# Turning k and r of one tile together: identity products on quarters of the TensorE array in place of whole-array transposes

## The chip, the cores and the metric

One core of a Trainium2 chip runs the whole program. The metric is the device time of one execution in microseconds (us), as the median of several runs.

## The reference, cut to what matters

Two blocks run one after the other. The first is an RWKV-6 recurrence over 4 batches, 8 heads, 768 steps and a head size of 48; the second is a layer norm with a two-layer MLP and a residual on the 384 joined head outputs.

```python
for t in range(S):                                  # S = 768
    cur = einsum('bhd,bhe->bhde', u * k[t], v[t])
    y[t] = einsum('bhd,bhde->bhe', r[t], state + cur)
    state = w[t][..., None] * state + einsum('bhd,bhe->bhde', k[t], v[t])
x = y as (B, S, 384)
xn = (x - mean) / sqrt(var + 1e-6) * g_ln
out = x + relu(xn @ w_ch1) @ w_ch2                  # 384 -> 1536 -> 384
```

All inputs and outputs are 32-bit floats.

## The kernel before, in words

The work is cut into eight **rounds** (4 batches by 2 halves of the sequence). A round has 384 steps, which are three tiles of 128 steps, for all 8 heads. Round 0 alone is cut again into a part of one tile and a part of two.

The **front** of a round (function `front`) is the attention. Step by step:

- `load` fetches w, k and r in their natural layout, with (position, head) on the 128 partitions.
- `inner` forms products of neighbouring steps on VectorE (DVE), GpSimd (POOL) and ScalarE (ACT). It leaves k and r in `pad_k` and `pad_r`: four steps s, three tiles c, two heads j of 64 columns each, of which 48 are used.
- `turn` (one call for k, one for r, for each tile c) brings k and r to the layout with the head dimension on the partitions. It issues four whole-array transposes of 128x112 numbers into one PSUM bank (`k_ps`, `r_ps`), and one ACT copy of 112x512 numbers into `k` or `r`. `turn_w` does the like for the decays (`w_ps`).
- `quads` forms the products r by k at four levels (lev 2 to 5), each 48 products of 48 rows on a quarter (64x64) of the array; `grow` scales k and r on DVE between the levels, and `keep` and `keep_last` copy the results into the matrix `A`. `place_own` puts the products inside a group of four steps there (the DVE rows `A<-mask_own,va`).
- `turn_k` turns k back (`kn_ps`). `states` forms k by v (24 products on quarters, `a<-v,k`) and the scan over states on DVE. `inside` multiplies `A` by v and `outputs` the states by r, both on quarters (`a<-v,A`, `a<-vx,A`, `a<-s,r`, `a<-last,r`).

The **back** of a round normalizes the output (`normalize`, `turn_x`: `xT_ps`) and runs the MLP (`mlp`). In round 0 the MLP uses plain 32-bit products (`h_ps<-xf,w`, `o<-ffn,h`). From round 1 on it splits each operand into parts (`h_ps<-xd,d`, `h_ps<-xhl,wl`, `h_ps<-xhl,wh`, and `second_product`: `a<-w2L,hL`, `o<-w2L,hL` and so on).

**PSUM** is shared out as two pairs of banks (the tag `a`, tiles a0 and a1, printed as `a_66` and `a_67`) and four single banks (the tag `b`). The pairs serve `quads`, `states`, `inside` with `outputs`, and two of the three output tiles of `second_product`, which hold a pair while the second product of a round runs. The single banks serve the transposes and `h_ps`.

**What sets the order.** All work is recorded as operations by `plan.add`, with an engine, an assumed cost, what is read and written, and whether it runs on quarters of the array (`tiled`). The class `Plan` then issues them in the sequence of the table `ORDER` (2246 numbers in one order for all engines; 10000 and more choose a second engine). The same function inserts products with zeros (`idle<-nought`) into PE's sequence where the assumed times leave PE without work. On each engine the order is thus fixed in the program; an instruction waits for semaphores where its inputs are not there. So the MLP of a round fills PE while the front of the next round waits for other engines.

Of the kernel before, what the change touches and what calls it, by code (L numbers as in the profile page):

```python
# [63 lines left out]
class Plan:  # L64
# [295 lines left out]
def kernel(  # L360
# [12 lines left out]
    nc = tc.nc  # L373
# [4 lines left out]
    B, H, S, D = r.shape  # L378
    P = 128
    HP = 64  # L380
# [1477 lines left out]
```

## Time and profile before

| what | value |
|---|---|
| median of 3 runs | 461.22 us (459.65 to 462.35) |
| the profiled execution, its own time | 460.29 us |
| its span in the trace | 458.5 us |
| granted TensorE clock, mean | 1.0 |
| instructions in the trace | 17709 |
| DVE busy | 365.9 us (80%) |
| ACT busy | 272.4 us (59%) |

The span runs from the first instruction of the program to the end of the last. PE is TensorE's products, PEld its weight loads, SP the engine that issues most DMAs. A row of a group gives the tile written, the tiles read, the sizes, the count, the busy time, and the mean duration of one in ns. A row of the timeline starts with the start and the length in us. For a matmul on PE the tile sizes are rows*columns of the weights that stand in the array, then the partitions and columns that stream. The length of a single matmul holds its way through the array, so the pace is read from starts and not from lengths.

### The profile page before, as it was taken

Reading aid. Unit: us, or ns where it says so; the run is one execution under the profiler, and the core shown is the slowest. Engines: PE = TensorE matmul, PEld = TensorE weight load, DVE = VectorE, ACT = ScalarE, POOL = GpSimd, SP = SyncE. Lnnn points to the kernel's source line nnn. Section 1 sums busy time; section 2 is a strip of 40 time slices with the busy share of each in tenths; the row PEclk is TensorE's granted clock in tenths of the full one; section 3 lists DMA queues with packets and bytes.
Section 4 is the critical chain, followed back from the end, with each engine's and each line's share of the span. In section 5 each row is a group of like instructions: output and inputs, shape, how many; then the busy total and the mean of one; then the engine's idle time right before and its main releaser. Section 6 shows DMA issues by size and latency. Waiting matters only on the chain.

```text
span 458.5 us, 17709 instructions
## 1 busy us (share of the span) xinstructions
PE 448.9 (98%) x7492; PEld 405.1 (88%) x7492; DVE 365.9 (80%) x791; ACT 272.4 (59%) x608; POOL 91.0 (20%) x112
## 2 busy tenths in 40 slices
PE   8999999999999999999999999999999999999996
PEld 4667888766899899989999999999999999999995
DVE  7999999999999989997899789679395666374524
ACT  5898789857665683735574544745634663464321
POOL 2226113232532641231026002210100010000000
PEclk9999999999999999999999999999999999999999
DMA  7877883784777758765755656463356525264541
GB/s 221 232 173 181 206 228 113 247 180 115 187 176 189 222 152 219 180 198 127 189 150 165 171 141 153 151 200 89 91 137 162 155 79 173 59 207 155 184 145 52
DMA packets 119201, 75.14 MB, mean 164 GB/s; under 512 B 63313, under 2 KB 116049, under 8 KB 119121
## 3 DMA queue, kind: packets, MB, share of 16 engines
q1 hardware_dynamic: 118848, 73.80, 59.1%
q8 instruction: 59, 0.97, 0.9%
q10 hardware_dynamic: 272, 0.20, 0.1%
q14 instruction: 22, 0.17, 0.1%
HBM read 61.79 MB, written 9.83 MB: 156 GB/s over the span
## 4 chain that ended last, share of the span: by engine, by line
PE 65%; DVE 4%; DMA 2%; issue 0%; ACT 0%; SPq 0%; DVEq 0%; ACTq 0%
PE a L47 27%; PE h_ps L47 25%; PE o L47 9%; PE xT_ps L47 1%; PE k_ps L47 1%; PE kn_ps L47 1%; PE r_ps L47 1%; DMA d<-w1d 1%; DMA va<-own_d 1%; DVE k L47 1%; DVE r L47 1%; DVE A L47 1%; DVE hL L47 1%; DVE w2L L47 0%; PE w_ps L47 0%
## 5 line engine op out<-in xcount | busy, mean ns | idle before, releaser
L47 DVE SCALAR_TENSOR_TENSOR hL<-h_ps,hH 128x384 fp32r<-128x384 f32 x84 | 45.8, 552 | 41.6 <-ACT hH L47 37.8
L47 ACT ACTIVATE hH<-h_ps 128x384 fp32r<-128x384 f32 x84 | 40.8, 489 | 56.8 <-PE h_ps L47 46.0
L47 ACT ACTIVATE h_ps<-h_ps 128x384 f32<-128x384 f32 x84 | 39.7, 481 | 52.4 <-PE h_ps L47 45.1
L47 PE MATMUL a<-w2L,hL 128*128 128x384 f32 x168 | 57.6, 344 | 0.1
L47 PE MATMUL h_ps<-xhl,wl 128*128 128x384 f32 x252 | 56.2, 332 | 0.0
L47 PE MATMUL h_ps<-xhl,wh 128*128 128x384 f32 x252 | 54.7, 326 | 0.0
L47 PE MATMUL a<-w2H,hH 128*128 128x384 f32 x168 | 54.7, 326 | 0.0
L47 PE MATMUL h_ps<-xd,d 128*128 128x384 f32 x252 | 53.6, 331 | 0.7 <-DMA d<-w1d 0.7
L47 PEld LDWEIGHTS a<-r,k 48*56 48x56 f32 (+3 forms) x3072 | 39.5, 122 | 12.5 <-issue 6.0
L47 DVE SCALAR_TENSOR_TENSOR hD<-hH,hL 128x384 fp32r<-128x384 f32 x84 | 44.5, 551 | 3.4 <-PE o L47 2.6
L47 PE MATMUL a<-r,k 48*56 48x32 f32 (+3 forms) x3072 | 44.1, 208 | 1.9 <-issue 0.5
L47 PEld LDWEIGHTS h_ps<-xd,d 128*128 128x128 f32 x252 | 42.1, 189 | 1.5 <-DVE pad_r L47 0.8
L47 PEld LDWEIGHTS h_ps<-xhl,wh 128*128 128x128 f32 x252 | 43.2, 189 | 0.0
L47 PEld LDWEIGHTS h_ps<-xhl,wl 128*128 128x128 f32 x252 | 42.4, 189 | 0.5
L47 PE MATMUL a<-w2s,hD 128*128 128x384 f32 x168 | 41.9, 341 | 0.2 <-DVE hD L47 0.2
L47 DVE TENSOR_TENSOR k<-k,tot 112x768 f32<-112x768 f32 (+1 forms) x40 | 32.5, 812 | 4.0 <-PE a L47 3.8
L47 DVE TENSOR_TENSOR r<-r,tot 112x768 f32<-112x768 f32 (+1 forms) x40 | 32.4, 814 | 1.2 <-PE a L47 1.2
L47 PEld LDWEIGHTS a<-w2L,hL 128*128 128x128 f32 x168 | 31.8, 189 | 0.6 <-DVE hL L47 0.4
L47 PEld LDWEIGHTS a<-w2H,hH 128*128 128x128 f32 x168 | 31.8, 190 | 0.0
L47 ACT COPY A<-a 32x384 f32<-32x384 f32 (+5 forms) x64 | 27.1, 427 | 5.9 <-DVE A L47 3.1
L47 PEld LDWEIGHTS a<-w2s,hD 128*128 128x128 f32 x168 | 27.8, 189 | 1.2 <-DVE hD L47 0.4
L47 PE MATMUL o<-w2L,hL 128*128 128x384 f32 x84 | 27.9, 332 | 0.0
(132 smaller groups left out, 973.8 us busy)
## 6 DMA issues: line engine op xcount, KB each, us to landing
d<-w1d SPq DMA_DIRECT2D x84, 192.0 KB, 3.3
w2s<-w2d SPq DMA_DIRECT2D x84, 192.0 KB, 3.4
raw<-in_moe_w_ch_dram SPq DMA_DIRECT2D x24, 384.0 KB, 4.4
nat_w<-in_w_dram SPq DMA_DIRECT2D x24, 192.0 KB, 3.9
nat_r<-in_r_dram SPq DMA_DIRECT2D x24, 192.0 KB, 3.5
v<-in_v_dram SPq DMA_DIRECT2D x24, 192.0 KB, 4.7
nat_k<-in_k_dram SPq DMA_DIRECT2D x23, 192.0 KB, 4.1
out_dram<-x SPq DMA_DIRECT2D x7, 576.0 KB, 3.6
```

The costliest lines, as they stand in the source:

```text
L47: ins = self.tc.keep_in_program_order(f(*args, **kw))
```

## The change

From round 1 on (`BOTH = 1`), `turn_both` takes the place of the two calls of `turn` for a tile. It takes a pair of banks (tag `a`) and not two single banks. For each of four steps s, for k and r, for the two halves i of the partitions and the two heads j, it issues one plain 32-bit product of 64 rows by 64 or 48 columns with a 64x64 piece of the identity: 32 products for a tile, on the four quarters of the array in turn. Partition half i writes bank i. After the last of them ACT copies k and r out of the pair, each with one copy of 112x512 numbers. Round 0 keeps `turn`. The table `ORDER` is a new one throughout.

```diff
-    THREE, FAST = 1, 1
+    THREE, FAST, BOTH = 1, 1, 1
...
+    def turn_both(part, c):
+        rnd, c0, nc = part
+        ps = f"kr_ps{rnd}_{c}"
+
+        def view():
+            t = tile_("a", ps, [P, 2, 512])
+            return t.rearrange("p i (m s n) -> p i m s n", m=2, s=Q)
+
+        def go():
+            t = view()
+            for s in range(Q):
+                for m, nm in enumerate("kr"):
+                    pad = tiles[f"pad_{nm}{rnd}"][:, s, c]
+                    for i in range(2):
+                        for j in range(2):
+                            PE.matmul(
+                                t[ds(HP * j, D if j else HP), i, m, s],
+                                pad[ds(C * i, C), j, 0 : D if j else HP],
+                                ident[ds(C * i, C), ds(C * i, C)], start=True, stop=True,
+                            )
+
+        def keep(m, nm):
...
+            ACT.copy(out=to, in_=view()[0:PD, :, m].rearrange("p i s (k a) -> p a i k s", a=NA))
...
+        plan.add(
+            "PE", 0.5, go, count=16 * Q,
...
+            pri=urgent(part, 5), lat=0.2, tiled=True,
+        )
...
         for c in range(c0, c0 + nc):
+            if rnd >= BOTH:
+                turn_both(part, c)
+                continue
             for nm in "kr":
                 turn(nm, part, c, 4 + "kr".index(nm))
...
     ORDER = [
-        2, 5, 3, 12, 4, 6, 13, 10, 14, 9, 8, 11, 16, 263, 17, 260, 18, 15, 7, 19, 10020, 27, 25, 261, 10021,
...
```

The new order is best seen in the instructions. **First place: PE in a later round, before.** The `outputs` of one round end, and the turns of the next stand one at a time between products of the MLP.

```order
L47 MATMUL h_ps_7_4675<-xhl_1_4312,wh_1_1222 128x384
L47 MATMUL h_ps_7_4675<-xhl_2_4198,wh_2_2019 128x384
L47 MATMUL k_ps_0_4844<-ident,pad_k 112x128 x4
L47 MATMUL a_66<-w2L_2385,hL_0_4849 128x384
L47 MATMUL a_66<-w2H_2045,hH_0_4699 128x384
L47 MATMUL a_66<-w2L_2385,hL_0_4849 128x384
L47 MATMUL a_66<-w2H_2045,hH_0_4699 128x384
L47 MATMUL o_2_4866<-w2L_2385,hL_0_4849 128x384
L47 MATMUL o_2_4866<-w2H_2045,hH_0_4699 128x384
L47 MATMUL h_ps_5_4869<-xd_4313,d_5_4855 128x384 x2
L47 MATMUL h_ps_5_4869<-xd_4199,d_5_4855 128x384
L47 MATMUL k_ps_1_4874<-ident,pad_k 112x128 x4
```

The same place of PE in the change:

```order
L47 MATMUL a_67<-s_4350,r_3415 64x48 x20
L47 MATMUL a_66<-s_4432,r_3415 64x48 x20
L47 MATMUL h_ps_5_4572<-xd_4098,d_5_4548 128x384 x2
L47 MATMUL h_ps_5_4572<-xd_4200,d_5_4548 128x384
L47 MATMUL a_67<-ident,pad_k 64x64
L47 MATMUL a_67<-ident,pad_k 48x64
L47 MATMUL a_67<-ident,pad_k 64x64
L47 MATMUL a_67<-ident,pad_k 48x64
L47 MATMUL a_67<-ident,pad_r 64x64
```

The last row begins the second of eight such groups of four; the 32 products of the tile follow each other. Then come six products of `h_ps`, and then the 64 products of the other two tiles. One product group of `h_ps` (three products) stands between the outputs in `a_67` and the turn that takes the same pair.

**Second place: PE near the start, before.** The names are those of round 0 (`v_409`, `k_192`, `A_83`) and of round 1 (`pad_k`); `xT_ps` belongs to the first part of round 0.

```order
L47 MATMUL a_67<-v_409,k_192 48x48 x16
L47 MATMUL xT_ps_1_0_726<-ident,xn_0_700 128x128
L47 MATMUL xT_ps_0_0_731<-ident,xn_0_700 128x128
L47 MATMUL idle<-nought 128x384 x2
L47 MATMUL idle<-nought 128x128
L47 MATMUL k_ps_0_741<-ident,pad_k 112x128 x4
L47 MATMUL k_ps_1_773<-ident,pad_k 112x128 x4
```

Behind these come the other turns of round 1, `inside` and `outputs` of the second part of round 0, and the first `h_ps`. In the change the turns of round 1 stand ahead of the last `a<-v,k` of round 0, and the stretch ends so:

```order
L47 MATMUL idle<-nought 128x128
L47 MATMUL a_66<-v_566,k_200 48x48 x16
L47 MATMUL xT_ps_1_0_907<-ident,xn_0_798 128x128
L47 MATMUL xT_ps_2_0_911<-ident,xn_0_798 128x128
L47 MATMUL idle<-nought 128x256
L47 MATMUL a_67<-r_801,k_803 60x32 x48
L47 MATMUL h_ps_6_0_970<-xf_0_967,w_2_0_111 128x128
```

The first `quads` of round 1 now stand ahead of the first `h_ps`, and `inside` and `outputs` of the second part behind it. The program has 34 products with zeros before (9728 columns in all) and 38 in the change (11520 columns).

**Third place: DVE near the start, before**, up to the first `place_own` of the first part of round 0 and behind it:

```order
L47 TENSOR_TENSOR k_192<-k_192,tot_189 112x2x4x32
L47 COPY_PREDICATED A_83<-mask_own,va_440 128x4x64
L47 ISA w_1_0_108<-w_1_0_108,held_96 128x768
L47 TENSOR_TENSOR k_192<-k_192,tot_189 112x2x4x32
L47 TENSOR_TENSOR pad_r<-nat_r,nat_w 128x6x2x48
L47 TENSOR_TENSOR pad_k<-nat_k,nat_w 128x6x2x48
L47 COPY s_590<-a_66 112x48 x2
```

The same place of DVE in the change:

```order
L47 TENSOR_TENSOR pad_k<-nat_k,nat_w 128x6x2x48
L47 TENSOR_TENSOR r_208<-r_208,tot_178 112x2x4x32
L47 TENSOR_TENSOR k_200<-k_200,tot_178 112x2x4x32
L47 TENSOR_TENSOR pad_r<-nat_r,nat_w 128x6x2x48
L47 TENSOR_TENSOR rk_0_568<-nat_k,nat_r 128x576
L47 COPY_PREDICATED A_83<-mask_own,va_563 128x4x64
L47 TENSOR_TENSOR r_208<-r_208,tot_178 112x4x2x32
L47 TENSOR_TENSOR nat_k<-nat_k,nat_r 128x1152
L47 TENSOR_TENSOR k_200<-k_200,tot_178 112x2x4x32
L47 ISA w_3_2_116<-w_3_2_116,held_104 128x768
L47 TENSOR_TENSOR nat_k<-nat_k,u_bc 128x1152
L47 COPY_PREDICATED A_83<-mask_own,va_563 128x4x64
```

The rows of 128x6x2x48, 128x576 and 128x1152 are the `inner` of round 1. In the change the two rows of 128x1152 stand ahead of the second `place_own` of the first part, and before behind it; `rk` of round 1 stands on DVE here and on POOL before.

More of the change, by code (lines that the diff above doesn't have):

```diff
@@ L759, in turn @@
         )
+    def turn_both(part, c):
[17 more added lines that the diff above has]
+        def keep(m, nm):
+            to = tile_(nm, f"{nm}{rnd}", [P, U, W])[0:PD].rearrange("p u (r t) -> p (u r) t", r=NP)
+            to = to[:, :, ts(c, P)].rearrange("p a (i k s) -> p a i k s", i=2, s=Q)
+            ACT.copy(out=to, in_=view()[0:PD, :, m].rearrange("p i s (k a) -> p a i k s", a=NA))
+        keys = {nm: keys_of(nm, (rnd, c, 1)) for nm in "kr"}
+        plan.add(
+            "PE", 0.5, go, count=16 * Q,
+            r=[(f"pad_{nm}{rnd}", i, c0) for nm in "kr" for i in range(2)] + keys["k"] + keys["r"], w=[ps],
+            new=[("a", ps)] + ([(nm, f"{nm}{rnd}") for nm in "kr"] if c == 0 else []),
+            pri=urgent(part, 5), lat=0.2, tiled=True,
+        )
+        for m, nm in enumerate("kr"):
+            plan.add(
+                "ACT", 0.587, lambda m=m, nm=nm: keep(m, nm), r=[ps], w=keys[nm],
+                pri=urgent(part, 5) + EVICT / 2, port=False,
+            )
     def turn_w(part):
```

257 rows, old and new, of the table ORDER are left out of this document.

## The prediction

> **What bounds the kernel now.** I read the page's busy times first, then four stretches of the span, then what PE waited for.
>
> ```profile
> span 458.5 us, 17709 instructions
> PE 448.9 (98%) x7492; PEld 405.1 (88%) x7492; DVE 365.9 (80%) x791; ACT 272.4 (59%) x608; POOL 91.0 (20%) x112
> PEclk9999999999999999999999999999999999999999
> ```
>
> PE is busy almost throughout and the granted clock is full, so neither a cold clock nor an idle PE is there to be won back late in the program. But a busy PE can be held up by its own pipeline or be filled with products of zeros. The stretches tell more:
>
> ```profile
> core 0: us, PE busy (x) PEld busy (x) DVE busy (x) ACT busy (x) POOL busy (x), PEclk, DMA share, GB/s
> 0.00:45.40 45.40, 41.91 (x792) 29.43 (x792) 41.97 (x114) 36.97 (x84) 16.60 (x32) 1.00 0.78 200
> 45.40:130.00 84.60, 83.87 (x1758) 67.69 (x1755) 82.37 (x180) 65.80 (x157) 21.98 (x25) 1.00 0.69 183
> 130.00:330.00 200.00, 198.95 (x3581) 188.15 (x3580) 170.92 (x350) 114.46 (x248) 49.63 (x49) 1.00 0.62 165
> ```
>
> Up to 45.4 us DVE works 42.0 us, and PE's busy time holds the products with zeros: DVE sets that stage. From there PE is full with real work; DVE is nearly full too until 130 us and has slack later. 45.4 us is where the first product of the MLP starts, after which no products with zeros follow, but one near the end:
>
> ```profile
> 37.98 1.68 PE L47 MATMUL idle<-nought 128*128 128x384 f32 x6
> 45.39 0.82 PE L47 MATMUL h_ps<-xf,w 128*128 128x128 f32 x5
> ```
>
> And PE, once it has work, waits for nothing long:
>
> ```profile
> PE k_ps L47 <- POOL pad_k L47: 1.3, 1, 1.3
> PE idle L47 <- DVE eps L47: 0.9, 1, 0.9
> PE h_ps L47 <- DMA d<-w1d: 0.7, 1, 0.7
> PE a L47 <- issue: 0.7, 3, 0.3
> ```
>
> These are the largest of eight, in us, times and longest; all eight together are under 5 us. So the time is the length of the first stage plus the work that PE has left behind it. The change touches both.
>
> **The products.** One tile's turns before, and their pace:
>
> ```profile
> L47 PE MATMUL k_ps<-ident,pad_k 128*112 128x128 f32 x96 | 14.5, 277 | 1.5 <-POOL pad_k L47 1.3
> L47 PE MATMUL a<-r,k 48*60 48x32 f32 x768 | 12.6, 217 | 0.5 <-issue 0.3 <-ACT k L47 0.2
> 171.00 0.60 PE L47 MATMUL k_ps<-ident,pad_k 128*112 128x128 f32 x4
> 171.44 0.60 PE L47 MATMUL r_ps<-ident,pad_r 128*112 128x128 f32 x4
> ```
>
> 24 tiles of four transposes are 96 records: one each. Four take 171.44 - 171.00 = 0.44 us, so k and r of a tile cost **0.88 us**. A level of `quads` has 48 products in each of eight rounds, 384, and stands with 768 records: a plain 32-bit product is two records. `turn_both` has no transposes, so its 32 products are **64 records**. The pace of records on quarters of the array:
>
> ```profile
> 19.92 1.08 PE L47 MATMUL a<-r,k 48*60 48x32 f32 x64
> 127.10 1.52 PE L47 MATMUL a<-r,k 48*60 48x32 f32 x96
> 156.06 0.25 PE L47 MATMUL a<-v,A 64*64 64x48 f32 x1
> 156.75 0.22 PE L47 MATMUL a<-vx,A 64*64 64x48 f32 x1
> 30.59 0.40 PE L47 MATMUL a<-v,k 64*48 64x48 f32 x16
> 149.29 0.76 PE L47 MATMUL a<-v,k 64*48 64x48 f32 x48
> ```
>
> With 60 columns of weights 32 more records take 0.44 us, 13.8 ns each. With 64 columns the first and the last of 48 (the second `inside` row is the 48th) start 0.69 us apart, 14.7 ns each. With 48 columns 32 more take 0.36 us, 11.3 ns. The pace goes by the columns of the weights. Here the head j = 0 has 64 and j = 1 has 48, but the quarters take turns, so the wider ones set the pace: 64 x 14.7 = **0.94 us** a tile. If each went at its own pace it would be 64 x 13.0 = 0.83 us. I take 0.94. A stream of 64 columns isn't shown on a quarter (the rows have 32 and 48); a whole-array transpose streams 128 columns in 0.11 us, so 64 columns on one of four quarters are 0.055 / 4 = 13.8 ns, still below the weights. So four quarters at once don't outweigh the doubled records: +0.06 us a tile. Rounds 2 to 7 have 18 tiles: **+1.1 us** (-0.9 to +1.1).
>
> **The stretches.** Going from the whole array to quarters and back costs time:
>
> ```profile
> 126.20 0.98 PE L47 MATMUL h_ps<-xd,d 128*128 128x384 f32 x5
> 128.56 0.76 PE L47 MATMUL h_ps<-xhl,wl 128*128 128x384 f32 x3
> 129.15 0.33 PE L47 MATMUL h_ps<-xhl,wh 128*128 128x384 f32 x1
> ```
>
> Products of 384 columns follow each other at 0.163 us. The five before the quads end their turn at 126.20 + 0.82 = 127.02; the three after them would have begun at 129.15 - 0.49 = 128.66 at that pace. The block took 1.65 us, of which 96 x 13.8 ns = 1.32 us are records: **0.33 us** for a stretch on quarters, whatever its length. Transposes of the whole array pay none of it. In the printed order of PE there are 76 such stretches before and 86 in the change, 60 and 68 of them behind the first product of the MLP: turns mostly stand alone or in twos, and the new order joins some other stretches. 8 x 0.33 = **+2.6 us**.
>
> **Work moved over the border of the stages.** `inside` and `outputs` of round 0's second part (64 products, 128 x 14.7 ns = 1.9 us) now stand behind the first product of the MLP, the first quads of round 1 (1.3 us) ahead of it, and the last product with zeros (0.2 us) is gone: **+0.4 us**.
>
> **The first stage.** It is DVE's, and the new order puts more of DVE's work ahead of round 0's first output:
>
> ```profile
> 31.72 0.46 DVE L47 COPY_PREDICATED A<-mask_own,va 128x256 f32<-128x256 int8 x1
> L47 DVE TENSOR_TENSOR nat_k<-nat_k,u_bc 128x1152 f32<-128x1152 f32 x7 | 9.4, 1349 | 0.0
> L47 DVE TENSOR_TENSOR nat_k<-nat_k,nat_r 128x1152 f32<-128x1152 f32 x5 | 6.7, 1350 | 1.1 <-ACT pad_k L47 1.1
> L47 DVE TENSOR_TENSOR rk<-nat_k,nat_r 128x576 f32<-128x576 f32 x4 | 3.0, 752 | 0.0
> ```
>
> The second `A<-mask_own,va`, at 31.72 us, lets `inside` of the first part start, and its norm and the MLP hang on that. Ahead of it stand now two rows of 128x1152 and one of 128x576 of round 1: 2 x 1.35 + 0.75 = 3.45 us more. Of smaller rows 1.9 us come and 2.0 us go. So **+3.3 us**. PE's own rows say the same: up to the first product of the MLP it has 3.1 us more products with zeros (1792 columns, two records, 0.11 us / 128 = 0.86 ns a column and record as in the transposes), 0.2 us more turns and two more stretches (0.7 us), less the moved 0.6: +3.4 us, if the zeros fill real waits. Bounds: 0, if DVE's later work in that stage shrinks as much, and +4.
>
> **ACT and the banks.** The two copies per tile have their old size:
>
> ```profile
> L47 ACT COPY k<-k_ps 112x512 f32<-112x512 f32 x24 | 14.0, 594 | 5.4 <-PE k_ps L47 5.4
> ```
>
> ACT has room, so their cost is hidden. But a tile now holds a pair of banks for 0.94 us of products and 2 x 0.59 us of copies, and during most of a round the second product holds the other pair. What is queued on PE behind a turn without a free pair is the MLP, in order, so PE stands still. Mostly six or more products of `h_ps` (1 us) or of the second product stand between. At two places one `h_ps` group (0.49 us) stands between `outputs` and the turn that takes its pair, and the rows show two copies of 0.4 us for such a pair:
>
> ```profile
> L47 ACT COPY x<-a 128x288 f32<-128x288 f32 x21 | 7.8, 419 | 3.7 <-PE a L47 3.6
> ```
>
> Twice 2 x 0.42 - 0.49 = 0.35 makes **+0.7 us**, from 0 to 4 us (six rounds with a wait as long as one copy of 0.59).
>
> **The sum.** 1.1 + 2.6 + 0.4 + 3.3 + 0.7 = 8.1 us. The profiled execution took 460.29 us, so 468.4; the median of the runs shown stands 0.9 us above it, so **469.3 us**.
>
> **Rivals.** *A product is one record.* If a product with the identity were one record as a transpose is, a tile would cost 32 x 14.7 = 0.47 us, 18 tiles 18 x (0.47 - 0.88) = -7.4 us and not +1.1, and the time 460.8. It decides below 0.48 us a tile, where the sum turns to zero; if the first stage then isn't later, the time is 457.5, **faster than before**. For it: a transpose is a product with the identity too, and is one record. Against it: every plain 32-bit group in the trace has two records a product, and nothing marks the identity. 0.08. [...]
>
> *Weights don't hide behind streams.* If a load and a stream followed each other, a record would cost 14.7 + 13.8 = 28.5 ns, a tile 1.82 us, and the time 469.3 + 18 x 0.88 = 485. Products j = 0 and j = 1 that follow each other share their partitions. Against it: `a<-v,k` has the same loop over i and j and runs at 11.3 ns a record, where load and stream in a row would be twice that. 0.03. [...]
>
> *The pairs block.* If PE waits for one copy of 0.59 us at each of some ten turns and quads, 5.9 us come on top: 475.2. For it: one pair is often held by the second product. Against it: the rows of the order show work between. 0.12.
>
> *The first stage stays where it is*: 469.3 - 3.3 = 466.0, and 464.0 if the quarters go at their own pace besides (18 x 0.11 = 2.0). For it: DVE's later rows of round 1 are done ahead. 0.12.
>
> **The numbers.** Forecast 0.65 (467 to 472), pairs 0.12, first stage 0.12, one record 0.08, loads 0.03. The range 464.0 to 475.5 leaves out the last two and the tails of the others. About half a per cent (2.3 us) is what a measurement of this kernel can tell from no change. One record gives "within" in 0.05 and "faster" in 0.03; some of the low side of the first-stage case, 0.02, is "within" too. Faster 0.03, within 0.07, slower 0.9.
>
> **What would show it.** In the profile after, `a<-ident,pad_k` and `a<-ident,pad_r` should have 1344 records together, and a lone turn should start its first and last record 0.93 us apart. Were there 672, the first rival is right. The first `h_ps<-xf,w` should start near 49 us; earlier means that the first stage was overrated. PE's waits should stay small apart from `a <- ACT`; if rows of PE waiting for k, r or x copies sum to over 3 us, the pairs block. I am wrong if the new order removes waits of DVE in the stretch from 45 to 130 us, where both engines are nearly full, by more than the products add.

## The result and the profile after

The changed kernel takes **482.69 us** (median of 3 runs, 479.29 to 485.38) against 461.22 us: 1.046 times as long, 95% interval 1.035 to 1.058, 21.5 us more. The forecast was 469.3 us with a range from 464.0 to 475.5: the direction was right, and the time lies 7 us above the range. The profiled execution is the one of 485.38 us, the slowest of the three, 25.1 us above that of before.

The rows of the page that answer to those of before, and the queue that brings instructions (packets, MB, share):

```profile
span 483.5 us, 20072 instructions
PE 463.6 (96%) x8676; PEld 413.6 (86%) x8676; DVE 368.3 (76%) x799; ACT 275.6 (57%) x613; POOL 85.4 (18%) x102
PEclk9989999998999999999998999999999999999999
q8 instruction: 68, 1.11, 0.9%
```

PE's busy share fell from 98% to 96% although it has more to do, and the clock has three dips where before has none. The same queue of the kernel before:

```profile
q8 instruction: 59, 0.97, 0.9%
```

2 x 8676 records (a load and a product each) on 68 packets are 255 for each packet, 2 x 7492 on 59 are 254, and a packet is 16 KB (1.11 MB on 68): TensorE's instructions come in **pieces of 256**. The three stretches of the span, for the kernel after:

```profile
0.00:45.40 45.40, 41.01 (x717) 27.62 (x719) 40.47 (x106) 36.78 (x81) 12.62 (x27) 0.96 0.78 219
45.40:130.00 84.60, 77.90 (x1968) 62.26 (x1961) 73.33 (x165) 60.48 (x146) 18.56 (x21) 0.98 0.58 144
130.00:330.00 200.00, 195.09 (x3905) 181.27 (x3897) 160.90 (x327) 105.13 (x228) 43.44 (x41) 0.99 0.59 160
```

From 45.4 to 130 us PE is busy 77.9 us (before 83.9) and DVE 73.3 (before 82.4): now neither is full. What PE waits for (us in total, times, longest):

```profile
PE a L47 <- issue: 7.9, 8, 2.6
PE h_ps L47 <- issue: 1.8, 1, 1.8
PE a L47 <- DVE r L47: 1.2, 2, 0.9
...
PE a L47 <- ACT a L47: 0.7, 1, 0.7
PE a L47 <- ACT r L47: 0.5, 1, 0.5
```

"Issue" is a wait in which no semaphore and no other engine is late. It was 0.7 us before and is **9.7 us** now; no other row is over 1.2 us. Two of these stops in PE's order of time (start, duration, what, how many; in brackets the idle time ahead):

```profile
102.68 2.10 PE L47 MATMUL o<-ffn,h 128*128 128x384 f32 x6
105.19 0.96 PE L47 MATMUL a<-r,k 48*32 48x32 f32 x91 [0.42 <-DVE k L47]
108.77 0.25 PE L47 MATMUL a<-r,k 48*32 48x32 f32 x5 [2.61 <-issue]
108.95 3.85 PE L47 MATMUL o<-ffn,h 128*128 128x384 f32 x6
...
255.77 0.59 PE L47 MATMUL h_ps<-xhl,wl 128*128 128x384 f32 x2
258.15 0.33 PE L47 MATMUL h_ps<-xhl,wl 128*128 128x384 f32 x1 [1.79 <-issue]
...
261.39 1.17 PE L47 MATMUL h_ps<-xhl,wh 128*128 128x384 f32 x3
```

Both stops stand in the midst of one group: 91 of the 96 records of a level of `quads` are done, then nothing for 2.61 us, then the last five, for which no semaphore and no engine is late. What moves in that time (queue 8 in the stretch from 105.9 to 107.4 us):

```profile
q8 instruction: 1, 0.02, 4.8%
```

That packet runs from 106.10 to 107.26 us in the trace, and PE goes on at 108.77, 1.5 us after its end. It set out 5.9 us after TensorE had begun the piece before it (at 100.23 us), where the median of the trace's packets is 1.4 us; why it set out so late no run shows.

That these are the ends of pieces can be counted. I number TensorE's instructions in the trace (loads, products and semaphore instructions) in order of their starts. The eight stops of `a <- issue`, the one of `h_ps <- issue` and one of 1.1 us at 133.6 us that has another name (shown at the end) all come right ahead of an instruction whose number leaves 193 or 194 when divided by 256. They are idle for 10.8 us together; before there are three such stops, 0.7 us together. The pieces that ran dry there are not mainly turns: products of `turn_both` stand in only three of the ten (138, 81 and 250 of the 256 instructions, 4.0 of the 10.8 us). The other seven hold `quads`, `inside`, `outputs` and the like, which the kernel before has too, in another order.

The first stop has a second price: `o<-ffn,h`, six records in 2.10 us ahead of it, takes 3.85 us for six behind it. The stretches of the second stop (us, PE busy and records, granted clock, DMA share, GB/s) say why:

```profile
256.10:258.10 2.00, 0.26 (x2) 1.00 0.41 106
258.10:262.40 4.30, 4.25 (x17) 0.61 0.92 275
```

For 4.3 us behind a stop of 1.8 us the clock is at 0.61 of full speed on the mean, and at 0.50 from 259.2 to 262.2 us. Behind the first stop it is at 0.50 from 108.95 to 111.95 us. Three of the ten stops have such a dip behind them (at 26, 109 and 258 us, idle for 0.9, 2.6 and 1.8 us); the others, of 0.4 to 1.1 us, have none.

For all of PE's time from its first product to its last I took each product at the pace that its shape has in the trace (0.163 us for 384 columns of a split operand, 14.7 ns for a record with 64 columns of weights on a quarter, 0.33 us a stretch on quarters) and what is late against that. The rows are an estimate by these paces:

| us | before | after | more |
|---|---|---|---|
| work at its pace | 418.5 | 423.4 | 4.9 |
| products with zeros (they fill planned waits) | 24.8 | 29.5 | 4.7 |
| stops that end 1.0 to 1.7 us after the end of a packet of instructions | 1.7 | 13.4 | 11.7 |
| other stops over 0.25 us | 1.3 | 2.2 | 0.9 |
| the rest: half clock and small gaps | 7.0 | 10.2 | 3.2 |
| sum | 453.3 | 478.7 | 25.4 |

There are 12 stops of the third kind after (4 before); 11 of them (3 before) stand at the end of a piece by the count above. The 13.4 us are more than the profile's 9.7, since the profile names a releaser for some of them and counts idle time alone. With the lateness of the products with zeros, all that is late comes to 17.5 and 34.6 us; the second is the number that the first expectation calls stops.

### The profile page after: what moved, and what is told of

The parts are those of the page before. It is cut to its first block, busy times and chain, and to the rows that moved or that the text cites. A ratio compares the mean times of both kernels' runs of the same rounds, so it can differ in the third digit from the quotient of the medians.

```text
span 483.5 us, 20072 instructions
## 1 busy us (share of the span) xinstructions
PE 463.6 (96%) x8676; PEld 413.6 (86%) x8676; DVE 368.3 (76%) x799; ACT 275.6 (57%) x613; POOL 85.4 (18%) x102
## 3 DMA queue, kind: packets, MB, share of 16 engines
q8 instruction: 68, 1.11, 0.9%
## 5 line engine op out<-in xcount | busy, mean ns | idle before, releaser
L47 PE MATMUL h_ps<-xhl,wl 128*128 128x384 f32 x252 | 57.3, 337 | 1.8 <-issue 1.8
L47 PEld LDWEIGHTS a<-r,k 48*60 48x60 f32 (+3 forms) x3072 | 40.1, 123 | 19.9 <-issue 12.1
L47 PE MATMUL h_ps<-xhl,wh 128*128 128x384 f32 x252 | 55.7, 331 | 0.0
L47 PE MATMUL h_ps<-xd,d 128*128 128x384 f32 x252 | 54.8, 335 | 0.4 <-DMA d<-w1d 0.4
L47 PE MATMUL a<-r,k 48*60 48x32 f32 (+3 forms) x3072 | 44.8, 210 | 8.9 <-issue 6.7
L47 DVE SCALAR_TENSOR_TENSOR hD<-hH,hL 128x384 fp32r<-128x384 f32 x84 | 45.4, 560 | 5.7 <-PE h_ps L47 3.6
L47 DVE TENSOR_TENSOR r<-r,tot 112x768 f32<-112x768 f32 (+1 forms) x40 | 31.4, 792 | 3.5 <-PE a L47 3.5
L47 ACT COPY A<-a 32x384 f32<-32x384 f32 (+5 forms) x68 | 29.0, 429 | 7.0 <-PE a L47 5.0
L47 PE MATMUL idle<-nought 128*128 128x384 f32 (+2 forms) x76 | 28.4, 499 | 0.9 <-DVE eps L47 0.9
```

What stands on the lines that cost most here:

```text
L47: ins = self.tc.keep_in_program_order(f(*args, **kw))
```

## The experiments

**Theory A**: a turn on quarters is 128 instructions in 0.94 us where it was 16 in 0.88; TensorE runs out of instructions, and its clock falls after the stop. **Theory B**: the new order makes it wait, whatever a turn is made of. **Theory C**: pairs of banks block.

### Whole-array transposes in the new order

```
-  for i in range(2): for j in range(2): PE.matmul(quarter i, j of pad, ident)
+  PE.transpose(t[0:PD, m, s], pad[:, 0:PD], ident)      # k to one bank, r to the other
```

> The changed kernel with its own order, pairs of banks and evictions, but each tile of k and r is turned by 8 whole-array transposes (4 of k into one bank of the pair, 4 of r into the other): 16 instructions for TensorE a tile where the products on quarters are 128. Theory A (TensorE starves for instructions, which come in pieces of 256, because a turn on quarters takes 128 of them in 0.94 us, and its clock falls after each stop): beside the 3.7 us that the products and their stretches cost by my forecast, some 10 to 15 us of stops and half clock go too: 464 to 470 us, TensorE's stops beyond 0.15 us fall from 34.6 us to some 20 us, and the two long ones near 108 and 258 us are gone. Theory B (the new order itself makes the engines wait, whatever the turns are made of): only the 3.7 us go, 477 to 481 us, and both long stops stay. Theory C (a turn that needs a pair of banks blocks or is blocked): as B, with waits for evictions ahead of the turns.

Measured: 1.026 (1.019 to 1.032) times before. That is some 473 us, 9 to 10 us under the changed kernel, between A and B. Once more, for its profile:

> The kernel with 8 transposes a tile into the pair of banks, in the changed kernel's order, once more, for an undisturbed profile. It took 473.5 us (9 us less than with products on quarters, 12 us more than the kernel before), so theory A (instructions) holds for some 5.5 us beyond the 3.7 us of the products, and the order or the pairs hold 12 us where I had forecast 4.4. A: the stops at ends of pieces near 108 and 258 us are gone. B (order): in this trace TensorE's waits, idle products and stops in the first 130 us still exceed those of the kernel before by 8 to 12 us in all. C (pairs): they lie right ahead of the turns, with an eviction as what ended them.

Measured: 472.9 us, 1.023 (1.020 to 1.026). PE's waits:

```profile
PE a L47 <- issue: 4.5, 5, 1.9
PE h_ps L47 <- DMA d<-w1d: 3.7, 4, 2.1
```

and where the MLP starts:

```profile
48.45 3.62 PE L47 MATMUL h_ps<-xf,w 128*128 128x128 f32 x30
```

The waits for instructions are half of those with products on quarters; work at its pace is 416.9 us, 6.5 less. The stop at 108 us is gone, but others stand elsewhere (1.9 us at 240). Waits for ACT's copies are 1.1 us in all, so C has nothing for it. But 11 us against the kernel before remain, in a form with no more work than it (416.9 against 418.5), so that part is not the turns on quarters. By B's own measure, idle gaps over 0.15 us and products with zeros in the first 130 us are 34.1 us against 27.2 before: 6.9 us more, a little under its 8 to 12.

### Half the instructions, the same order

```
-  t[ds(HP * j, ...), i, m, s], pad[ds(C * i, C), j, 0:...]   # 32 products, 64 records
+  t[0:PD, i, m, s], pad[ds(C * i, C), 0:PD]                 # 16 products, 32 records
```

> The changed kernel with its order, where each product with the identity covers a half of the array's rows and all 112 columns at once instead of a quarter: 16 products, 64 instructions a tile instead of 128, same values, same banks. The turn's own time is unknown for this shape: 0.43 us a tile if the two halves run beside each other at 13.5 ns a record, 0.86 us if one after the other, so 0 to 11 us less work over the 21 tiles. Theory A (instructions): the stops shrink by at least half of the extra 17 us, on top of that work: 460 to 474 us. Theory B (order): 471 us (halves beside each other) to 482 us (one after the other), with both long stops as they were.

Measured: 486.1 us, 1.054 (1.048 to 1.059). Both expected times are missed, for a reason of its own. One lone turn:

```profile
48.30 0.41 PE L47 MATMUL a<-ident,pad_k 64*112 64x64 f32 x4
48.55 0.36 PE L47 MATMUL a<-ident,pad_r 64*112 64x64 f32 x4
...
49.73 0.36 PE L47 MATMUL a<-ident,pad_r 64*112 64x64 f32 x4
```

Four records take 0.20 us, 49.4 ns each: 1.53 us from the first record to the last, over the upper bound of 0.86 that I gave, an estimate for a shape that no run had shown. Whether the two halves run beside each other this doesn't tell: two records of 112 columns of weights in 2 x 49.4 ns are 0.88 ns a column, and four of 64 columns on the quarters in 4 x 14.7 ns are 0.92. Work at its pace is 436.8 us, 13.4 more than in the changed kernel, and yet the time is only 3.4 us longer. The waits:

```profile
PE a L47 <- issue: 1.7, 3, 1.2
PE h_ps L47 <- issue: 0.8, 1, 0.8
```

2.5 us instead of 9.7, in the same order, and the two long stops, which B expected to stay, are gone: A's part by the waits, not by the time.

### Twice the instructions

```
+  for _ in range(2):        # around all products of a turn
```

> The changed kernel with each turn's products on quarters made twice over into the same places (256 instructions a tile instead of 128; same values). The added products are 21 times 0.94 us = 19.7 us of work in stretches that are there already. Theory A: a turn then eats a whole piece of 256 instructions in 1.9 us, about half of the 3.7 us between two pieces, so a stop of up to 1.8 us follows nearly every turn and more half clock with it: 515 to 535 us, and TensorE's stops rise by over 10 us. Theory B: about 482.7 + 19.7 = 502 us, stops as before.

Measured: 519.55 us, 1.123 (1.116 to 1.129): 36.9 us more than the changed kernel for 19.7 us of work. B's 502 us is out.

```profile
PE a L47 <- issue: 18.5, 13, 2.5
```

Nearly twice as much, and eleven stops of over 0.25 us of idle time stand inside a turn, where the changed kernel has one.

### One record for each product

This kernel leaves out the turning of k and r but for the first product of each; it only keeps the shapes and places of the others.

```
+  one = s + i + j > 0
+  one_r[rows, 0:n] if one else pad[rows, j, 0:n],  one_r[rows, rows] if one else ident[rows, rows]
```

> The changed kernel with its order, where of the 32 products of a turn only the first of k and the first of r stay as they are; the other 30 have the same shapes and places but 16-bit zeros for both operands, so that each is one record instead of two (k and r of rounds 1 to 7 are zero but for a sixteenth part: this leaves their turn out and keeps its instructions). A tile then has 34 records, 68 instructions, near the 64 for which the order was found, instead of 64 and 128. At 14.7 ns a record it takes 0.50 us instead of 0.94, so 21 times 0.44 = 9.2 us of work go in any case. Theory A (instructions): the stops at ends of pieces fall as in the form with halves, from 13.4 us to some 4, and some 3 us of half clock behind them too: 458 to 464 us, at the time of the kernel before or under it. Theory B (order): only the 9.2 us go: 471 to 475 us, stops at ends of pieces over 10 us.

Measured: 468.67 us, 1.011 (1.005 to 1.017): 14.0 us less than the changed kernel, of which 9.3 us are work at its pace (414.1). The rest is between the two expectations.

```profile
PE a L47 <- issue: 2.5, 2, 1.5
PE h_ps L47 <- issue: 1.0, 2, 0.7
```

Waits for instructions fell from 9.7 to 3.5 us. Part of it came back as other stops (5.2 us instead of 2.2).

### The ends of the pieces moved in the kernel before

```
+  for _ in range(32): PE.matmul(t[0:32, 0:32], zeros[:, 0:32], ...)    # warm-up, once
+  n -= 10
```

> The kernel before, in whose warm-up 10 units of idle products of 128 columns are replaced by 32 products of 32 by 32: 116 more instructions for TensorE ahead of the first real one, about the same time, nothing else changed. Theory A: the ends of the pieces of 256 instructions fall 116 instructions earlier in the whole program, at places for which the order was not found: 1 to 4 us slower (462 to 465 us), with stops at some ends of pieces where the kernel before has none. Theory B or C: no change beyond 0.3% (461 us).

Measured: 463.35 us, ratio 1.002 (0.999 to 1.005): not told from no change.

```profile
PE a L47 <- issue: 3.3, 5, 1.0
PE h_ps L47 <- issue: 0.3, 1, 0.3
```

The waits rose from 0.7 to 3.6 us, as A has it; by the time alone this run decides nothing.

### The order found anew for the turn's true size

`turn_both` is entered in the planner as 64 instructions and 0.5 us. Here it gets its true numbers, and ORDER is searched anew by the planner's own sum.

```
-  "PE", 0.5, go, count=16 * Q,
+  "PE", 0.95, go, count=32 * Q,
```

> The changed kernel with its turn entered in the planner at its true size (128 instructions, 0.95 us, instead of 64 and 0.5) and an order searched anew from the changed kernel's own, for the same planner. The planner's own end goes from 467.8 (the order on record, true size) to 459.3. Theory A: stops at ends of pieces and the half clock behind them go, as they do with transposes: 470 to 476 us, stops beyond 0.15 us down from 34.6 to some 22 us. Theory B: the order was found for turns half as long as they are, so engines wait for late turns: the same gain, but by shorter waits and idle products in the first 130 us, with stops at ends of pieces as before. If neither (products on quarters slow what is beside them): 479 us or more.

Measured: 481.58 us, 1.043 (1.037 to 1.048): no gain that can be told, where A and B both had one (the third range, 479 us or more, is the one that was met). The form with transposes, with its own numbers and order:

> 8 transposes a tile into the pair of banks, entered as 16 instructions and 0.874 us, with an order searched anew from the changed kernel's (the planner's own end goes from 460.0 to 454.5; the kernel before stands at 451.9 there). Theory A and B: what is left against the kernel before is what the pairs themselves cost, about 3 us: 463 to 467 us. Theory C (pairs block in a way that the planner doesn't know): 470 us or more, as with the changed kernel's order.

Measured: 475.52 us, 1.032 (1.025 to 1.038), not under the 472.9 us of the changed kernel's order. Waits for instructions of the two:

```profile
PE a L47 <- issue: 6.3, 9, 1.4
```

```profile
PE a L47 <- issue: 5.0, 5, 1.7
PE h_ps L47 <- issue: 0.3, 1, 0.3
```

The planner's own end had fallen to 459.3 and 454.5 us with these orders. So my belief that the wrong numbers in the planner were the cause, and the right ones the cure, falls. A search that allows for ends of pieces that are not quite where they are counted:

> The changed kernel, its turn entered at its true size, with an order searched anew as in the run before with products on quarters, but over five displacements of the ends of pieces (up to 36 instructions either way) at once. In the planner the order of that earlier run is sharp: 459.3 where the ends lie as counted, 462 to 464 with the ends 12 to 36 instructions elsewhere, which would explain its 6.3 us of waits for instructions on the chip. The new one stays within 460.1 and 461.7 over all of these. Theory A (the waits come from where the ends of pieces fall): TensorE's waits for instructions at most 3 us, and 472 to 478 us; the rest against the kernel before is TensorE's work on quarters, the longer first stage and the pairs. Theory B (the turns on quarters lack instructions wherever the ends fall): waits for instructions of 6 us or more again, 479 us or more.

Measured: 481.57 us, 1.044 (1.038 to 1.049).

```profile
PE a L47 <- issue: 4.1, 7, 0.9
PE h_ps L47 <- DMA d<-w1d: 3.2, 2, 2.1
...
PE idle L47 <- issue: 0.8, 1, 0.8
```

> 8 transposes a tile into the pair of banks, with an order searched anew over the same five displacements (the planner's end 454.3 to 455.2 over all of them). Theory A: waits for instructions at most 2 us instead of 4.5 and 5.3, and 464 to 470 us. Theory B: 473 us or more, as with the two orders before.

Measured: 471.51 us, 1.019 (1.015 to 1.024).

```profile
PE a L47 <- issue: 1.9, 1, 1.9
...
PE h_ps L47 <- issue: 0.4, 1, 0.4
```

The waits for instructions go down to 4.9 us (A's bound was 3) and 2.3 us (A's bound was 2), but other waits come in their place (in the first 3.2 us for a weight tile from DRAM), and both times miss A's ranges upwards; the first time, but not its waits, is what B had.

### The kernel before, in other orders

What is an order worth that is as good in the planner and was only never run? Only ORDER is changed.

> The kernel before, unchanged but for its order: some 6000 random steps led it away and a search over displaced ends of pieces brought the planner's end back to 451.9 (451.9 to 452.3 over the displacements; the order on record 451.9 to 453.3). 373 of TensorE's 594 entries stand elsewhere. Theory D (an order that is only as good in the planner costs several us on the chip against the order on record, by waits and ends of pieces that the planner doesn't see): 465 to 470 us, so that the same share of the changed kernel's 21.5 us is its new order as such, and with transposes in pairs most of the 10 us. Against D (orders that are equal in the planner are equal on the chip): 459 to 463 us, and those 10 us are what the pairs and the later first stage cost.

> As the run before it, from another random walk (planner's end 451.7; 406 of TensorE's 594 entries elsewhere). The same two expectations; that both agree tells whether one order was a chance.

Measured: 475.49 us, 1.025 (1.019 to 1.031), and 468.33 us, 1.014 (1.008 to 1.019). Their waits:

```profile
PE h_ps L47 <- DMA d<-w1d: 3.9, 1, 3.9
PE a L47 <- DMA w2s<-w2d: 3.5, 4, 1.8
PE a L47 <- issue: 1.8, 2, 1.4
```

```profile
PE xT_ps L47 <- ACT xn L47: 3.8, 1, 3.8
PE h_ps L47 <- DMA d<-w1d: 2.8, 1, 2.8
...
PE a L47 <- issue: 1.2, 1, 1.2
```

Theory D holds, the first time even above its range: the old form, with its old work (418.4 us at its pace in both), loses 11 and 6 us by another order. The rows show the largest of it as single late transfers and one late result of ACT, and the granted clock is 0.989 in both profiled executions where it was 1.0 (that of the second is its slowest, 473.0 us). The three orders with transposes in pairs lose 9 to 15 us by their ratios, so most of that needs no price of the pairs; some 3 or 4 us for them are not excluded.

### The ends of the pieces moved in the changed kernel

Form and order stay; in the warm-up products with zeros are exchanged for smaller ones.

```
+  for _ in range(18): PE.matmul(t[0:32, 0:32], zeros[:, 0:32], ...)    # 36, 52
+  n -= 6                                                               # 12, 15
```

> The changed kernel, in whose warm-up 6 of the first 15 units of idle products are replaced by 18 products of 32 by 32: 64 more instructions ahead of the first real one, about the same time, the same order behind it. If it is where the ends of pieces fall: TensorE's waits for instructions differ from 9.7 us by 3 us or more in at least one of the three runs with displaced ends, the stops stand at other instructions, and the time moves by 3 to 8 us with them. If turns of 128 instructions starve TensorE anywhere: 8 to 12 us of such waits and 479 to 486 us in all three.

> As the run with 64, with 12 units replaced by 36 products: 128 more instructions ahead of the first real one. The same two expectations.

> As the run with 64, with all 15 units replaced by 52 products: 188 more instructions ahead of the first real one. The same two expectations.

Measured: **477.60 us** (1.035, 1.030 to 1.040), **487.28 us** (1.055, 1.052 to 1.058) and **487.44 us** (1.052, 1.047 to 1.057). Waits for instructions, in this order:

```profile
PE a L47 <- issue: 4.9, 7, 1.3
PE h_ps L47 <- issue: 1.2, 2, 0.8
```

```profile
PE a L47 <- issue: 9.2, 10, 2.1
...
PE idle L47 <- issue: 0.5, 1, 0.5
```

```profile
PE a L47 <- issue: 8.6, 9, 1.7
```

The first turn starts at 8.86 to 9.02 us in all three (8.89 in the changed kernel), so the warm-up itself costs the same; work at its pace is 423.4 us in each, as in the changed kernel. One and the same order differs by 9.8 us by where the pieces end. The stops stand at other products of the program, but counted as above all of those with the name `issue` again come ahead of number 193 or 194 of 256, in all three runs. So it is the place of the ends, for the size of the loss. But in none of the four places do the waits go below 6 us, where the old form shows 0.7 and 3.6. The waits alone do not order the times (9.7 us go with 482.7 and with 487.3); the granted clock adds to them. In the profiled executions of 477.7, 485.4, 488.5 and 487.9 us (the changed kernel is the second) its mean is 0.999, 0.989, 0.985 and 0.982, which by span and clock is an estimated 0.5, 5.3, 7.3 and 8.7 us lost.

| | instructions a turn | waits for instructions, us | time, us |
|---|---|---|---|
| twice | 256 | 18.5 | 519.6 |
| changed kernel; ends moved by 64, 128, 188 | 128 | 9.7; 6.1, 9.7, 8.6 | 482.7; 477.6, 487.3, 487.4 |
| one record | 68 | 3.5 | 468.7 |
| halves | 64 | 2.5 | 486.1 |
| transposes in the pair | 16 | 4.5 | 472.9 |

From 68 instructions a turn downwards the waits show no clear further fall (3.5, 2.5 and 4.5 us): a part of them goes with the order, whatever a turn is made of.

## Why the prediction was wrong

**Products: right.** 1344 records were forecast and came (four groups of 336). A lone turn:

```profile
46.84 0.34 PE L47 MATMUL a<-ident,pad_k 64*64 64x64 f32 x8
...
47.66 0.33 PE L47 MATMUL a<-ident,pad_r 64*48 64x64 f32 x8
```

The first record starts at 46.84 us and the last at 47.77: 0.94 us in the trace (936 ns), as forecast, so one record for a product and weights that don't hide are both out.

**Stretches: right.** The work at its pace rose by 4.9 us; the forecast has 1.1 for the products, 2.6 for the stretches behind the first product of the MLP, 0.7 for two ahead of it and 0.2 of turns, 4.6 in all.

**First stage: nearly right, hidden by the stops.** With transposes in the same order the first `h_ps<-xf,w` starts at 48.45 us, 3.1 us later than before; "near 49" was forecast. In the changed kernel it starts late:

```profile
52.41 0.82 PE L47 MATMUL h_ps<-xf,w 128*128 128x128 f32 x5
```

Of the 4 us between the two, 2.2 are longer stops at ends of pieces (1.1, 0.3 and 1.3 us, at 26, 46 and 51 us, against 0.6). Products with zeros rose by 4.7 us in all, where the forecast had 3.1 for the first stage.

**Pairs of banks: right that they are small.** PE's waits for ACT's copies are 1.2 us in all (0.7 had been forecast), under the 3 us that would have spoken for blocking.

**The step that failed** is the first reading: "So the time is the length of the first stage plus the work that PE has left behind it", with the forecast that "PE's waits should stay small". The terms of that sum came out at 9.6 us (4.9 and 4.7) for 8.1. What it lacks is everything that is neither: 11.7 us of stops at ends of pieces (9.0 us by the profile's own row), 3.2 us of half clock and small gaps, 0.9 us of other stops, 15.8 us of the 25.4. I costed a record by its 14.7 ns alone. But each record is a load and a product, two instructions, and a tile's turns went from 16 instructions to 128 in the same time, 7.3 ns each. The profile of before had the two rows that would have asked the question: `issue: 0.7` among PE's waits, which I passed over as small, and queue 8 with 59 packets. The turns are only part of it. The sum took the new order to cost nothing but its first stage, and most of the stops stand where that order puts the end of a piece behind other products on quarters (seven of ten, 6.8 of 10.8 us idle).

**How the 21.5 us divide.** Quarters against transposes in one order: 482.7 - 472.9 = 9.8 us, of which 6.5 are work and stretches, and the rest waits for instructions and clock, less a wait for DMA that is 3.3 us longer with the transposes. The other 11.7 us stand in a form with no more work than before. Two other orders of the old form lose 7.1 and 14.3 us by their medians against 461.2 (6 and 11 by the ratios to the runs beside them), so an order as such can account for most of it, and the later first stage of this one (3.1 us) is part of that. That it does so here is argued from those two orders and not shown.

**What stays open**: whether turns on quarters have an order that is free of these waits on the chip. The best of six tries (four places of the ends, two orders) is 477.6 us. No version here beats the kernel before. Why the same binary varies more where it waits for instructions (479 to 485 us against 460 to 462) was not tried by itself; the granted clock goes with it (0.996, 0.992 and 0.989 in the executions of 479.3, 482.7 and 485.4 us, by span and clock an estimated 3.4 of the 6.1 us between first and last). Open too is why some packets set out late, as that of the longest stop did.

## What to carry to other kernels

Where a change trades few long instructions for many short ones, count the instructions as well as the time: a stretch that eats 256 of them faster than a piece arrives can stop (here 128 instructions of a turn took 0.94 us, and no two pieces set out less than 3.3 us apart), at a place that depends on everything ahead of it, and the clock can fall behind the stop (to 0.50 behind three of the ten stops here). Look for waits in the midst of a group of like products, released by "issue", before you blame a dependency; number the instructions and see whether the stops lie a multiple of 256 apart, and test it by moving the ends of the pieces with a few tiny products in the warm-up. And where a planner sets the order, a new form comes with a new order: run the old form in another order too, before a difference of a few per cent is put down to the form.

## What the runs showed of the hardware

- Instructions of TensorE come in packets of 16 KB for 256; in the trace of the changed kernel no two of them start less than 3.3 us apart (the ten closest pairs 3.3 to 3.7 us), most take 0.9 to 1.5 us, and PE goes on 1.1 to 1.7 us after the end of one it waited for (ten stops, all at the same number within 256, give or take one).
- A stop inside one operation's products can carry a wrong name. At 133.6 us the turn stops between two groups of its own products, 1.1 us after a packet's end, and the row names a tile that no product of it reads:

```profile
132.19 0.31 PE L47 MATMUL a<-ident,pad_k 64*48 64x64 f32 x8
133.59 0.34 PE L47 MATMUL a<-ident,pad_r 64*64 64x64 f32 x8 [1.09 <-DVE vals L47]
```

- 64 rows by 112 columns of weights run at 49.4 ns a record, where 64 by 64 run at 14.7 ns: a half does what two quarters do, in 49.4 ns instead of 29.4.
- In the run with one record for each product, 30 products of a turn with 16-bit operands stand with one record each (630 records on 21 tiles). The 34 records of a turn, four of them with 32-bit operands, took 439 ns, 13.3 ns a record, where the same shapes with 32 bits alone run at 14.7 ns.
